# Scaling q and k by the decay factors on GpSimd instead of VectorE, in a fused retention and two-layer feed-forward kernel

## The chip, the cores and the metric

The kernel runs on one core of a Trainium2 chip. A core has five engines with instruction queues of their own: TensorE (PE in the profile; PEld is its weight load), VectorE (DVE), ScalarE (ACT), GpSimd (POOL) and SyncE (SP, which here only issues DMAs). Each engine takes its instructions strictly in the order of its queue, and an instruction that waits for a semaphore holds everything queued behind it. The metric is the device time of one execution in microseconds (us), as the median of several runs.

## The reference

```
scores = q @ k.T / sqrt(64)                    # q, k, v: (4 batches, 8 heads, 576, 64), float32
gamma  = 1 - 2 ** (-5 - arange(8))             # one decay per head
D[i,j] = gamma ** (i - j) if i >= j else 0
x      = ((scores * D) @ v)                    # heads side by side: (2304, 512)
h      = x @ w_in1;  g = where(h > 0, h, exp(min(h, 0)) - 1);  y = g @ w_out1     # 512 -> 2048 -> 512
h      = maximum(y @ w_in2, 0);                out = (h * h) @ w_out2
```

The weights arrive as float64.

## The kernel before, in words

The 2304 tokens are cut into five blocks (512, 512, 256, 512 and 512 tokens), and the blocks into 20 chunks of at most 128 tokens that don't cross a batch: 4, 5, 2, 5 and 4 chunks. The decay gamma^(i-j) is split into a factor for the query and one for the key, so each chunk's q and k (token by 8 heads by 64) are multiplied once by a table `cs` before anything else is done with them: this is `scale_chunk`, L261 to L269, two TENSOR_TENSOR instructions of 128x512 (or 64x512) in place for each chunk. In the kernel before, the 4 chunks of the first block are scaled on GpSimd and the other 16 on VectorE.

A chunk then goes through three pieces (`attn_pieces`). `transposes` turns q and k on TensorE into PSUM (`ps_t`, L293), and ScalarE copies them out (`qT`, `kT`, L298). `scores` multiplies them (`ps_s`, L306), and VectorE applies the causal mask (`P`, L309). `values` adds the state of the earlier chunks (`ps_o`, L321) and the products with v (L325); ScalarE and VectorE split the result into a high and a low part `x` (L159, L160); the state `st` is brought up to date from `ps_u` (L335, L341, L343).

All large products are made of three float32r products of high and low parts (`mm3`, L163 to L165). The first layer is `up` (`h`, then L365 to L370 and the split of `g`) and `down` (`acc`). Its weights are turned from float64 to float32 on the chip (`to_f32`, L204 and L205 on ScalarE, L206 to L211 on VectorE) and split (`w`, L159 and L160). Blocks 0 and 1 share each weight tile as it is made, so that from 14 us to about 90 us of the trace the attention of blocks 0 and 1, the making of the weights and the first products lie side by side. The attention of blocks 2, 3 and 4 is spread between the products of blocks 1 to 3, up to some 410 us. The second layer follows (`A`, `D`, L492; then `m`, L675); no scaling is done in it.

q, k and v of a chunk come in by DMAs from SP's queue (L256) into buffers that two chunks share in turn; a load waits there until the chunk two before is through with its buffer.

The order of each engine's instructions isn't the order of the source: a scheduler sorts them when the kernel is built, by priorities and its own model of when each engine is free. Taking instructions off one engine therefore moves others on all engines.

Of the kernel before, what the change touches and what calls it, by code (L numbers as in the profile page):

```python
# [85 lines left out]
def chunks_of_blocks():  # L86


    out = []
    for t, n in BLOCKS:  # L90
        end, cs = t + n, []
        while t < end:
            b, s = divmod(t, S)
            n = min(P, S - s, end - t)
            cs.append((b, s, n))
            t += n
        out.append(cs)
    return out
# [6 lines left out]
def scale_cols(s):  # L105
    c = C_S + 2 * H * STARTS.index(s)
    return c, c + H
# [19 lines left out]
def tile_kernel(ctx: ExitStack, tc, q, k, v, w_in1, w_out1, w_in2, w_out2, cst, out):  # L127
    nc = tc.nc
# [109 lines left out]
    blocks = chunks_of_blocks()  # L238
# [22 lines left out]
    def scale_chunk(ch):  # L261
        n = ch[2]
        qn, kn, _ = nat[ch]

        eng = nc.gpsimd if ch in blocks[0] else nc.vector
        for t, c in zip((qn, kn), scale_cols(ch[1])):
            eng.tensor_tensor(
                out=t[:n], in0=t[:n], in1=cs[:n, c:c + H].unsqueeze(2).to_broadcast([n, H, D]), op=ALU.mult
            )  # L269

# [450 lines left out]
    def scale_next():  # L721
        if at["scale"] < at["load"]:
            scale_chunk(chunks[at["scale"]][0])
            at["scale"] += 1
# [184 lines left out]
```

## Time and profile before

| | |
|---|---|
| median of 3 runs | 890.87 us (886.36 to 891.96) |
| the profiled execution | 890.54 us, of which the span of the profile is 888.7 us |
| TensorE busy | 857.8 us, 97% of the span |
| VectorE busy | 685.7 us, 77% |
| ScalarE busy | 490.6 us, 55% |
| GpSimd busy | 8.7 us, 1%, 12 instructions |

TensorE is busy nearly all the time, so what counts are the stretches in which it has to wait, or runs at a lower clock. Busy shares are means over stages that differ; the rows below are taken from the stages in which the scaling is done.

### The profile page before, as it was taken

To read this page: it belongs to the slowest core of one execution; us is meant where nothing else is said; L and a number is where in the kernel's file an instruction comes from. 1 tells how busy PE (TensorE), PEld (TensorE's weight loads), DVE (VectorE), ACT (ScalarE), POOL (GpSimd) and SP (SyncE) were. 2 spreads that over 40 slices of the span, in tenths; PEclk is the share of its full clock that TensorE was granted. 3 is DMA by queue.
4 is the path that set the end of the run, shared out by engine and by line. 5 is a ranking of instruction groups with operands and counts; after the bars stand their busy time and mean duration, and the time that the engine had idled before them with its cause. 6 is when DMAs were issued, how large, how long until landed. Compare 5 with 4: busy or idle time off the path is not lost.

```text
span 888.7 us, 14956 instructions
## 1 busy us (share of the span) xinstructions
PE 857.8 (97%) x5630; PEld 771.3 (87%) x5630; DVE 685.7 (77%) x1391; ACT 490.6 (55%) x961; POOL 8.7 (1%) x12
## 2 busy tenths in 40 slices
PE   7898999999998999999999999999999989999998
PEld 5686888888887988888888898999989989999997
DVE  4998888885666868766778867789884769898984
ACT  3674778673464656555767744556553434444441
POOL 3000000000000000000000000000000000000000
PEclk9999899999999999999999999999999999999999
DMA  9944306383529656533462034499998994444330
GB/s 226 276 107 160 96 24 190 119 214 95 142 63 221 163 157 185 187 107 131 142 225 95 25 104 157 154 328 332 348 319 281 401 345 137 160 146 144 120 131 37
DMA packets 157608, 155.33 MB, mean 175 GB/s; under 512 B 62816, under 2 KB 121312, under 8 KB 157536
## 3 DMA queue, kind: packets, MB, share of 16 engines
q1 hardware_dynamic: 150208, 139.69, 51.9%
q10 hardware_dynamic: 7328, 14.68, 4.6%
q8 instruction: 44, 0.72, 0.3%
q14 instruction: 28, 0.23, 0.1%
HBM read 98.77 MB, written 55.57 MB: 174 GB/s over the span
## 4 chain that ended last, share of the span: by engine, by line
PE 73%; DVE 10%; DMA 9%; issue 3%; ACT 2%; SPq 2%; ACTq 0%; DVEq 0%
PE m L675 18%; PE acc L163 7%; PE acc L164 7%; PE acc L165 7%; PE h L163 7%; PE h L164 6%; PE h L165 6%; PE A L492 5%; PE D L492 3%; DMA k<-in_k_dram 2%; DMA f<-w2s 2%; PE ps_o L325 2%; DVE go L519 1%; DMA wo2s<-wo 1%; PE ps_o L321 1%
## 5 line engine op out<-in xcount | busy, mean ns | idle before, releaser
L675 PE MATMUL m<-wo,S 128*128 128x256 f32 x1512 | 183.8, 284 | 3.6 <-ACT S L159 3.6
L675 PEld LDWEIGHTS m<-wo,S 128*128 128x128 f32 x1512 | 183.3, 193 | 4.0 <-ACT S L159 4.0
L159 ACT CAST S<-g 128x512 fp32r<-128x512 f32 (+1 forms) x144 | 75.3, 565 | 94.2 <-DVE g L659 45.6
L163 PE MATMUL h<-x,w 128*128 128x512 f32 (+1 forms) x320 | 120.3, 378 | 3.4 <-DVE t L370 2.4
L165 PE MATMUL h<-x,w 128*128 128x512 f32 (+1 forms) x320 | 118.8, 371 | 0.0
L164 PE MATMUL h<-x,w 128*128 128x512 f32 (+1 forms) x320 | 118.7, 371 | 0.0
L164 PE MATMUL acc<-g,w 128*128 128x512 f32 (+1 forms) x320 | 118.5, 371 | 0.0
L165 PE MATMUL acc<-g,w 128*128 128x512 f32 (+1 forms) x320 | 117.5, 370 | 0.0
L492 PE MATMUL A<-T,pair 128*128 128x384 f32 x576 | 113.4, 336 | 1.5 <-DVE go L519 0.8
L163 PE MATMUL acc<-g,w 128*128 128x512 f32 (+1 forms) x320 | 111.4, 375 | 2.2 <-DVE x L402 1.3
L492 PEld LDWEIGHTS A<-T,pair 128*128 128x128 f32 x576 | 100.5, 188 | 4.0 <-DVE go L519 2.3
L160 DVE TENSOR_TENSOR S<-g,S 128x512 fp32r<-128x512 f32 (+1 forms) x144 | 86.4, 621 | 22.7 <-ACT S L159 20.9
L365 ACT ACTIVATE t<-h 128x512 f32<-128x512 f32 (+1 forms) x80 | 44.3, 554 | 82.5 <-PE h L165 78.9
L369 DVE SCALAR_TENSOR_TENSOR t<-e,t 128x512 f32<-128x512 f32 (+1 forms) x80 | 50.8, 635 | 49.3 <-ACT t L367 49.0
L163 PEld LDWEIGHTS h<-x,w 128*128 128x128 f32 x320 | 60.6, 190 | 15.5 <-DVE t L370 3.4
L159 ACT CAST g<-t 128x512 fp32r<-128x512 f32 (+1 forms) x80 | 46.2, 578 | 47.0 <-DVE t L370 45.2
L163 PEld LDWEIGHTS acc<-g,w 128*128 128x128 f32 x320 | 59.4, 188 | 13.4 <-DVE x L402 1.7
L165 PEld LDWEIGHTS h<-x,w 128*128 128x128 f32 x320 | 60.7, 190 | 10.6 <-DVE w L160 0.2
L164 PEld LDWEIGHTS h<-x,w 128*128 128x128 f32 x320 | 60.7, 190 | 10.2
L164 PEld LDWEIGHTS acc<-g,w 128*128 128x128 f32 x320 | 60.3, 188 | 10.2
L165 PEld LDWEIGHTS acc<-g,w 128*128 128x128 f32 x320 | 60.2, 188 | 10.1
L492 PE MATMUL D<-T,pair 128*128 128x384 f32 x288 | 58.5, 336 | 1.7 <-DVE pair L160 1.1
(88 smaller groups left out, 1279.3 us busy)
## 6 DMA issues: line engine op xcount, KB each, us to landing
g2s<-go SPq DMA_DIRECT2D x48, 384.0 KB, 4.4
g<-g2s SPq DMA_DIRECT2D x36, 512.0 KB, 3.7
raw<-in_moe_w_in_dram SPq DMA_DIRECT2D x32, 512.0 KB, 5.6
raw<-in_moe_w_out_dram SPq DMA_DIRECT2D x32, 512.0 KB, 4.3
wo2s<-wo SPq DMA_DIRECT2D x56, 256.0 KB, 4.2
wo<-wo2s ACTq DMA_DIRECT2D x9, 1536.0 KB, 14.8
w2s<-f SPq DMA_DIRECT2D x32, 256.0 KB, 2.2
f<-w2s SPq DMA_DIRECT2D x32, 256.0 KB, 3.9
```

The costliest lines, as they stand in the source:

```text
L159: nc.scalar.copy(pair_hi, src)
L160: eng.tensor_tensor(out=pair_lo, in0=src, in1=pair_hi.bitcast(F32), op=ALU.subtract)
L163: nc.tensor.matmul(ps, l_hi, r_hi, start=first, stop=False)
L164: nc.tensor.matmul(ps, l_hi, r_lo, start=False, stop=False)
L165: nc.tensor.matmul(ps, l_lo, r_hi, start=False, stop=last)
L321: i = nc.tensor.matmul(ps[:, p, :n], st[:, p, :], qT[:, p, :n], start=p == 0, stop=True, skip_group_check=True)
L325: nc.tensor.matmul(ps[e * D:(e + 1) * D, p, :n], vn[:n, 2 * p + e, :], live[e][:n, p, :n], start=not s, stop=True, skip_group_check=True,)
L365: nc.scalar.activation(t, h, AF.Relu, scale=-1.0)
L369: nc.vector.scalar_tensor_tensor(out=t, in0=e, scalar=1.0, in1=t, op0=ALU.add, op1=ALU.mult)
L492: ins = nc.tensor.matmul(ps, w[:, l, o:o + P], t[:, r, j], start=first and i + j == 0, stop=i + j == 3, skip_group_check=True)
L519: nc.vector.tensor_tensor(out=out, in0=by3(x), in1=by3(y), op=ALU.add)
L675: ins = nc.tensor.matmul(m(u, k), l[:, x], w[:, y], start=first and k in (1, 6, 4, 5), stop=j == HF - 1 and i == 2, skip_group_check=True,)
```

## The change

The choice of an engine goes, and all 20 chunks are scaled on GpSimd:

```diff
-        eng = nc.gpsimd if ch in blocks[0] else nc.vector
         for t, c in zip((qn, kn), scale_cols(ch[1])):
-            eng.tensor_tensor(
+            nc.gpsimd.tensor_tensor(
                 out=t[:n], in0=t[:n], in1=cs[:n, c:c + H].unsqueeze(2).to_broadcast([n, H, D]), op=ALU.mult
             )
```

32 instructions leave VectorE's queue and stand in GpSimd's, behind the 8 that were there, in the order of the chunks. The file is one line shorter from here on, so L293 of the kernel before is L292 of the changed one, and so on.

What follows are pieces of the order of instructions, without times. The first is TensorE's, where the third chunk of block 1 gets its scores (`ps_s`, at 68.45 us of the trace) and its values (`ps_o`, at 70.39 us), among the products of the first layer. Before:

```order
L164 MATMUL acc_732<-g,w_435 128x512
L165 MATMUL acc_732<-g,w_435 128x512
L164 MATMUL acc_733<-g,w_435 128x512
L165 MATMUL acc_733<-g,w_435 128x512
L306 MATMUL ps_s<-qT,kT 128x128 x8
L321 MATMUL ps_o<-qT,st 128x128 x4
```

and after:

```order
L164 MATMUL acc_732<-g,w_435 128x512
L305 MATMUL ps_s<-qT,kT 128x128 x8
L165 MATMUL acc_732<-g,w_435 128x512
L164 MATMUL acc_733<-g,w_435 128x512
L165 MATMUL acc_733<-g,w_435 128x512
L320 MATMUL ps_o<-qT,st 128x128 x4
```

Three products of the first layer now stand between the scores and the values.

The second is TensorE's too, between the values of the fourth chunk of block 1 and the transposes of its fifth (at 86.05 us of the trace). Before:

```order
L335 MATMUL ps_u<-v,k 64x64 x8
L165 MATMUL acc_730<-g,w_706 128x512
L165 MATMUL acc_731<-g,w_706 128x512
L165 MATMUL acc_732<-g,w_706 128x512
L165 MATMUL acc_733<-g,w_706 128x512
L293 MATMUL ps_t<-cs,q 128x64 x4
L293 MATMUL ps_t<-cs,k 128x64 x4
```

and after:

```order
L164 MATMUL acc_733<-g,w_706 128x512
L165 MATMUL acc_730<-g,w_706 128x512
L165 MATMUL acc_731<-g,w_706 128x512
L165 MATMUL acc_732<-g,w_706 128x512
L165 MATMUL acc_733<-g,w_706 128x512
L320 MATMUL ps_o<-qT,st 128x128 x4
L324 MATMUL ps_o<-P_789,v 64x128
```

Four products (L165) that stood between the values with their state (`ps_o`, `ps_u`) and the next transposes now stand ahead of the values, and the transposes follow right behind `ps_u`.

The third is VectorE's, in block 2's products, around 297 to 302 us of the trace; `t` (L369, L370) is the activation of the first layer, `k` a chunk of block 3 that is scaled. Before:

```order
L160 TENSOR_TENSOR x<-ps_o,x 128x4x128
L341 TENSOR_TENSOR st<-ps_u,st 64x4x64 x2
L369 SCALAR_TENSOR_TENSOR t<-e,t 128x256
L267 TENSOR_TENSOR k<-k,cs 64x512
L370 TENSOR_TENSOR t<-h,t 128x256
L206 TENSOR_SCALAR f<-f 128x512
```

and after:

```order
L160 TENSOR_TENSOR x<-ps_o,x 128x4x128
L340 TENSOR_TENSOR st<-ps_u,st 64x4x64 x2
L368 SCALAR_TENSOR_TENSOR t<-e,t 128x256
L369 TENSOR_TENSOR t<-h,t 128x256
L206 TENSOR_SCALAR f<-f 128x512
```

The scaling is gone from between the two steps of the activation; nothing has come in its place.

## Rows read from the trace of the kernel before

**Rows 1.** Busy time by stretches: length, then each engine; PEclk is TensorE's granted clock.

```profile
30.00:70.00 40.00, 38.14 (x276) 31.34 (x276) 38.77 (x74) 24.84 (x46) 0.00 (x0) 0.96 0.64 164
70.00:92.00 22.00, 18.08 (x190) 14.89 (x192) 16.33 (x32) 10.52 (x21) 0.00 (x0) 0.95 0.47 156
92.00:97.00 5.00, 5.00 (x20) 3.91 (x17) 4.83 (x11) 2.96 (x6) 0.00 (x0) 0.54 0.00 0
...
760.00:888.70 128.70, 124.41 (x1037) 124.21 (x1036) 104.40 (x239) 51.90 (x100) 0.00 (x0) 1.00 0.36 119
```

**Rows 2.** TensorE's timeline, 40 to 92 us: start, length, what, [idle before, releaser].

```profile
44.79 0.47 PE L163 MATMUL h<-x,w 128*128 128x512 f32 x1 [0.54 <-DVE t L370]
...
70.39 1.16 PE L321 MATMUL ps_o<-qT,st 128*128 128x128 f32 x8 [0.78 <-DVE P L309]
...
79.93 0.50 PE L163 MATMUL acc<-g,w 128*128 128x512 f32 x1 [0.77 <-ACT w L159]
...
86.05 0.43 PE L293 MATMUL ps_t<-cs,q 64*128 64x64 f32 x4 [0.51 <-DVE x L160]
...
89.12 1.36 PE L321 MATMUL ps_o<-qT,st 128*128 128x64 f32 x8 [1.03 <-DVE P L309]
```

**Rows 3.** TensorE's timeline, 280 to 302 us.

```profile
280.26 0.66 PE L293 MATMUL ps_t<-cs,q 128*128 128x128 f32 x4 [1.33 <-DVE x L160]
...
288.76 0.38 PE L163 MATMUL h<-x,w 128*128 128x256 f32 x1 [0.71 <-DVE t L370]
...
301.94 0.39 PE L163 MATMUL h<-x,w 128*128 128x256 f32 x1 [0.48 <-DVE t L370]
```

**Rows 4.** The scaling's own line: count, duration in ns min/median/max, first and last start.

```profile
L267 DVE TENSOR_TENSOR q<-q,cs x16: 677/684/694, 32.1 to 360.4; 128x512 f32<-128x512 f32 x12, 64x512 f32<-64x512 f32 x4
...
L267 POOL TENSOR_TENSOR spare<-spare,cs x6: 1042/1044/1140, 8.7 to 21.1; 128x512 f32<-128x512 f32 x6
```

**Rows 5.** VectorE's timeline, 16 to 21 us.

```profile
16.47 0.74 DVE L206 TENSOR_SCALAR f<-f 128x512 f32<-128x512 f32 x1
17.13 0.68 DVE L309 TENSOR_TENSOR spare<-ps_s,cs 128x512 f32<-128x512 f32 x1
17.73 0.93 DVE L208 SCALAR_TENSOR_TENSOR f<-raw,f 128x512 int32<-128x512 int32 x1
...
19.80 0.91 DVE L211 CUSTOM_DVE_ANT_0 f<-raw,f 128x1024 uint16<-128x1024 uint16 x1
```

**Rows 6.** GpSimd's timeline in the same stretch.

```profile
15.88 2.22 POOL L267 TENSOR_TENSOR spare<-spare,cs 128x512 f32<-128x512 f32 x2 [4.93 <-DMA spare<-in_q_dram]
19.11 1.04 POOL L267 TENSOR_TENSOR spare<-spare,cs 128x512 f32<-128x512 f32 x1 [1.01 <-DMA spare<-in_q_dram]
```

**Rows 7.** Two lines' durations on VectorE, L206 and L208, as in rows 4.

```profile
L206 DVE TENSOR_SCALAR f<-f x64: 405/419/737, 14.5 to 457.0; 128x512 f32<-128x512 f32 x64
...
L208 DVE SCALAR_TENSOR_TENSOR f<-raw,f x64: 673/685/925, 17.7 to 458.4; 128x512 int32<-128x512 int32 x64
```

**Rows 8.** Waits over the whole span: total us, times, longest.

```profile
DVE k L267 <- DMA k<-in_k_dram: 9.1, 7, 3.5
...
DVE q L267 <- DMA q<-in_q_dram: 7.2, 5, 2.7
```

**Rows 9.** VectorE's timeline, 278 to 302 us.

```profile
278.91 0.69 DVE L267 TENSOR_TENSOR q<-q,cs 128x512 f32<-128x512 f32 x1 [2.65 <-DMA q<-in_q_dram]
...
285.23 0.68 DVE L267 TENSOR_TENSOR q<-q,cs 64x512 f32<-64x512 f32 x1 [1.85 <-DMA q<-in_q_dram]
...
300.75 0.68 DVE L267 TENSOR_TENSOR k<-k,cs 64x512 f32<-64x512 f32 x1 [2.16 <-DMA k<-in_k_dram]
301.46 0.42 DVE L370 TENSOR_TENSOR t<-h,t 128x256 f32<-128x256 f32 x1
```

**Rows 10.** TensorE's timeline, two products in a row.

```profile
66.77 0.39 PE L165 MATMUL acc<-g,w 128*128 128x512 f32 x1
67.00 0.39 PE L164 MATMUL acc<-g,w 128*128 128x512 f32 x1
```

## The prediction

> **What bounds the kernel now.** I read the profile in this order: busy time by stretches, TensorE's timeline for its gaps, the scaling's own line, the waits, and then both sides of the first 25 us, the one place where GpSimd and VectorE work side by side.
>
> TensorE bounds the kernel; VectorE matters only where TensorE waits for it. There are two such places. From 30 to 92 us VectorE is busy 38.8 of 40 us and then 16.3 of 22 us [rows 1], and TensorE's gaps end on it, directly or through a weight that it finishes: 0.54, 0.78, 0.77, 0.51 and 1.03 us [rows 2]; with one more like the 0.77 (0.74 us, at 73.77) and one of 0.46 us (at 87.40), neither shown, that is 4.83 us. Right behind them, from 92 to 97 us, the granted clock is 0.54, so TensorE runs there at its lower level, 1.2 of 2.4 GHz, most of the time: 5 us times 0.46 makes 2.3 us lost [rows 1]. Before it fell, TensorE had stopped three times within 4 us. The second place is block 2's products, where gaps of 1.33, 0.71 and 0.48 us end on VectorE [rows 3], 2.5 us together.
>
> So all that VectorE could give back is 4.83 + 2.3 + 2.5 = 9.6 us, 1.1% of the profiled execution's 890.54 us (its span, 888.7 us, and 1.84 us around it). It lies 0.33 us under the median of the three runs, 890.87 us, so a sum against it needs no correction. The three runs lie 5.6 us apart, and about 1%, 8.9 us, is what a measurement of this kernel can tell from no change.
>
> **Taken off VectorE.** 32 instructions, 16 for q and 16 for k [rows 4]: ten for block 1's five chunks, from 32.1 us on, the others in the products of blocks 1 to 3. One takes 0.68 us, but gives way to the next after 0.60 us, as the one of 0.68 us at 17.13 does to that at 17.73 [rows 5]: 6.0 us in the first place, 13.2 us later.
>
> **Put on GpSimd.** The same work takes 1.04 us there [rows 4]; behind the first block's 8 nothing else stands in that queue, which is idle from then on. Such an instruction can start as soon as its DMA has landed; on VectorE it stood in line. The path from a load to the transposes gets longer by 0.36 us (1.04 less 0.68) where TensorE waits for the load itself, which I see only at 280.26.
>
> **What the two do to each other.** This is the price that decides. Two GpSimd instructions run from 15.88 to 18.10 us and one from 19.11 to 20.15 [rows 6]. Beside them VectorE's L206 takes 0.74 us, L208 0.93 and L211 0.91 [rows 5], where the medians of L206 and L208 are 0.42 and 0.685 [rows 7], and L211 is taken to be as long as L208; both L208 and L211 end 0.56 us after GpSimd's end (18.66, 20.71). So they were held until GpSimd was through, and then ran. L309, which takes one input from PSUM, starts at 17.13 in the middle of the pair and keeps its 0.68 us: it isn't held. In the weights' conversion and the activation most instructions are of the first kind (L206, L207, L208, L211, the splits of `w` and `g`, L369). One GpSimd instruction therefore costs VectorE between 0, where it meets nothing of that kind, and 1.04 us, where it holds VectorE for all its time. The rows' own mean: L206 lost 0.32, L208 0.24 and L211 some 0.22 us, together 0.78 over three GpSimd instructions, 0.26 each. VectorE had free time there; in a full queue I take 0.6, between the mean of the rows and the upper end. Against the 0.60 that the instruction cost VectorE itself this is nothing: ten times (0.60 less 0.6) is 0 us in the first place. The ends are 3.4 us won, at 0.26 each, and 4.4 us lost, at 1.04 each.
>
> The Trainium skill, SBUF — State Buffer, section "SBUF: two separate sides", puts this as an exclusive lock: a VectorE instruction with two SBUF inputs, or in a two-port mode, and a GpSimd instruction exclude each other, and the later one waits for the whole of the other. The rows above agree, L309's too. By it the 0.6 would stand nearer to 1.04, and the first place would lose up to 4.4 us, which is the second rival.
>
> **The waits in VectorE's queue that go.** While VectorE waits for a load of q or k, all its other work stands behind: 9.1 us for k and 7.2 us for q [rows 8]. Three of those show in TensorE's gaps. At 285.23 it had stood 1.85 us for q, and at 300.75 it had stood 2.16 us for k with L370 right behind it, at 301.46 [rows 9], for which TensorE then waited, 0.71 and 0.48 us [rows 3]. In the new order nothing stands between the two steps of the activation; both gaps should go: 1.2 us. The wait at 278.91, 2.65 us [rows 9], holds up the split of `x`, and with it the transposes at 280.26. But these need the same q, which GpSimd has at 278.91 + 1.04 = 279.95 at the earliest, so only some 0.2 of that 1.33 us goes. The other 22 instructions of that stage meet a VectorE with free time and cost nothing that TensorE sees. Gain: 1.2 + 0.2 = 1.4 us.
>
> **What the new order moves.** At 70.39 TensorE waits 0.78 us for the masked scores. Three products now lie between scores and values; in a row they start 0.23 us apart [rows 10], 0.69 us: gain 0.7 us. At 86.05 the opposite: four products (0.9 us) that covered the way from values over `x` to the next transposes now stand ahead of the values. They are done either way, but the way itself lies open: I expect the gap of 0.51 us to grow, and count 0.4 us lost net, since the values' own wait at that place gets shorter. The dip of the clock behind it then stays, 0 us. The other gaps of the first place I leave as they are: the 0.77 comes from weights that were made late, and VectorE gets no faster by the balance above.
>
> The order also changes in the last stage (from 760 us), where nothing is scaled. TensorE's idle time there is 4.3 of 128.7 us [rows 1]; another order can take some of that away or double it, 4 us to either side; I count 0.
>
> **Sum:** 890.54 - 1.4 - 0.7 + 0.4 = 888.8 us. Its own range is 883 to 895: the ends of the first place and of the last stage reach 4 us or so to either side each, and are hardly met together, so some 6 us to either side.
>
> **First rival: VectorE's relief counts.** If GpSimd's instructions meet mostly work that they don't hold, VectorE's queue in the first place is shorter by up to 6 us, the weights come in time, the stops from 70 to 90 us go and with them the fall of the clock: up to 9.6 us, 881 us. For it: the rows' mean of 0.26 us, and a VectorE 97% busy ahead of these gaps. Against it: several of the gaps are not a matter of load but of a chain (scores, mask, values), and most of VectorE's work there is of the kind that is held.
>
> **Second rival, slower: the lock in a full queue.** If nearly every GpSimd instruction holds VectorE to its end, each costs 1.04 instead of 0.60: ten times 0.44, 4.4 us, in the stretch from 30 to 92 us, in which VectorE has 1.2 us to spare in the first 40. TensorE waits for the weights and masks that come later; a further stop or two brings a second fall of the clock like that at 92 us, 2.3 us; and of the 22 later ones half meet a busy activation, 11 times 0.44, 4.8 us. Together 11.5 us, 902 us. It decides from the point at which the mean hold exceeds 0.60 us by more than VectorE's free time, 1.2 us over ten, so from 0.72 us each. For it: L208 and L211 were held to the very end. Against it: the waits for loads leave VectorE's queue, and the later stage has room.
>
> That the change does something else than it says is excluded by the order: all 32 stand on GpSimd.
>
> **How the numbers follow.** The forecast gets 0.66, the first rival 0.15, the second 0.19; each rival may fall some 5 us to either side of its time. Faster by over 1% is under 882.0 us: two thirds of the first rival's share and 0.02 of the forecast's, 0.12. Slower by over 1% is over 899.8 us: three quarters of the second rival's share, 0.14. Within 1%: 0.74. From 881 to 901 us leaves out half of the first rival and a little over half of the second, 0.18, and holds all of the forecast.
>
> **What would show it.** In the profile after: 40 GpSimd instructions of L267, of about 1.05 us each, and a GpSimd busy time near 42 us. VectorE's L206 to L211 with longest times near 1.5 us and a higher mean, most of all between 30 and 80 us; if their means stay, the first rival holds. No wait of VectorE for q or k; no gaps of TensorE at L163 behind L370 in block 2's products. The gap between scores and values of block 1's third chunk under 0.2 us, that before its fifth chunk's transposes longer. A second stretch with a clock near 0.5 would speak for the second rival. The prediction is wrong if GpSimd's instructions themselves wait long for VectorE, so that TensorE waits for transposes, or if the last stage changes by more than 4 us.

## The result, and the profile after

The changed kernel takes 895.61 us (median of 7 runs, 893.31 to 898.71); the kernel before, run on the same chip, takes 889.96 us (7 runs, 886.36 to 892.68). The ratio is 1.007, with a 95% interval from 1.005 to 1.009; a second set of runs gave 1.0053 (1.0035 to 1.0072). It is slower by some 5 us, where 888.8 us, slightly faster, was forecast. The time lies 0.6 us beyond the forecast's own range, 883 to 895, and within the wider one, 881 to 901; the sign is wrong. The profiled execution took 893.66 us, with a span of 891.9 us. It is among the fastest of the seven and 3.1 us above that of the kernel before, so the two profiles side by side show only a part of the loss.

In the changed kernel all line numbers from 265 on are one less, so the scaling is L266 and the activation's two steps are L368 and L369. Busy time by stretches, which answers to [rows 1], with one wider stretch around the fall of the clock:

```profile
30.00:70.00 40.00, 36.45 (x251) 29.92 (x252) 36.52 (x62) 23.86 (x44) 15.18 (x9) 0.92 0.62 161
70.00:92.00 22.00, 18.87 (x179) 14.96 (x177) 17.65 (x30) 10.81 (x20) 1.63 (x2) 0.98 0.47 156
92.00:97.00 5.00, 4.27 (x43) 4.02 (x42) 2.28 (x6) 1.18 (x3) 0.00 (x0) 0.50 0.00 0
...
86.00:110.00 24.00, 21.44 (x153) 17.98 (x152) 17.93 (x35) 15.07 (x29) 0.00 (x0) 0.79 0.18 64
```

The last stretch in the kernel before:

```profile
86.00:110.00 24.00, 22.43 (x133) 18.64 (x134) 19.89 (x38) 17.23 (x33) 0.00 (x0) 0.86 0.26 72
```

From 30 to 70 us TensorE has lost 1.7 us of busy time (36.45 for 38.14), VectorE is less busy, and the clock still falls at 92 us. TensorE's timeline names the gaps, as in [rows 2] and [rows 3]:

```profile
38.48 0.50 PE L164 MATMUL h<-x,w 128*128 128x512 f32 x1 [0.31 <-DVE x L160]
...
45.15 0.66 PE L292 MATMUL ps_t<-cs,q 128*128 128x128 f32 x4
47.15 0.63 PE L292 MATMUL ps_t<-cs,k 128*128 128x128 f32 x4 [1.34 <-ACT qT L297]
48.51 0.50 PE L163 MATMUL h<-x,w 128*128 128x512 f32 x1 [0.73 <-DVE t L369]
...
82.95 0.50 PE L163 MATMUL acc<-g,w 128*128 128x512 f32 x1 [0.52 <-ACT w L159]
...
89.38 0.43 PE L292 MATMUL ps_t<-cs,q 64*128 64x64 f32 x4 [1.04 <-DVE x L160]
90.15 0.43 PE L292 MATMUL ps_t<-cs,k 64*128 64x64 f32 x4 [0.33 <-DVE st L340]
...
92.75 1.97 PE L320 MATMUL ps_o<-qT,st 128*128 128x64 f32 x8 [0.73 <-DVE P L308]
...
284.28 0.66 PE L292 MATMUL ps_t<-cs,q 128*128 128x128 f32 x4 [1.24 <-POOL q L266]
...
286.17 0.66 PE L292 MATMUL ps_t<-cs,k 128*128 128x128 f32 x4 [0.29 <-POOL k L266]
...
292.69 0.39 PE L163 MATMUL h<-x,w 128*128 128x256 f32 x1 [0.64 <-DVE t L369]
```

The place to look at is 47 to 48.5 us. Before, TensorE transposed q there, waited 0.54 us at 44.79 and went on with `h`'s products; k's transposes came 12 products later. TensorE's timeline of the kernel before:

```profile
43.60 0.66 PE L293 MATMUL ps_t<-cs,q 128*128 128x128 f32 x4
...
47.64 0.60 PE L293 MATMUL ps_t<-cs,k 128*128 128x128 f32 x4
```

Now k's four transposes stand right behind q's. They wait 1.34 us until ScalarE has copied qT out, and then `h` waits 0.73 us for the activation: 2.07 us for 0.54. The gap of 0.78 us at 70.39 is gone, as forecast, and so is the one at 301.94.

The scaling's own line now stands on GpSimd (minimum, median, maximum in ns):

```profile
L266 POOL TENSOR_TENSOR q<-q,cs x17: 1037/1109/2616, 4.6 to 364.7; 128x512 f32<-128x512 f32 x13, 64x512 f32<-64x512 f32 x4
L266 POOL TENSOR_TENSOR k<-k,cs x17: 1039/1138/4648, 6.4 to 371.1; 128x512 f32<-128x512 f32 x13, 64x512 f32<-64x512 f32 x4
```

VectorE's timeline, changed kernel. In the first three rows it is held by GpSimd; the other seven are what it does while TensorE stands at 47 us:

```profile
31.39 1.27 DVE L206 TENSOR_SCALAR f<-f 128x512 f32<-128x512 f32 x1
...
34.73 1.52 DVE L160 TENSOR_TENSOR w<-f,w 128x512 fp32r<-128x512 f32 x1
36.17 1.53 DVE L208 SCALAR_TENSOR_TENSOR f<-raw,f 128x512 int32<-128x512 int32 x1
...
44.97 0.41 DVE L206 TENSOR_SCALAR f<-f 128x512 f32<-128x512 f32 x1
45.31 0.67 DVE L211 CUSTOM_DVE_ANT_0 f<-raw,f 128x1024 uint16<-128x1024 uint16 x1
45.91 0.67 DVE L368 SCALAR_TENSOR_TENSOR t<-e,t 128x512 f32<-128x512 f32 x1
46.51 0.41 DVE L207 TENSOR_SCALAR f<-f 128x512 int32<-128x512 int32 x1
46.85 0.67 DVE L160 TENSOR_TENSOR w<-f,w 128x512 fp32r<-128x512 f32 x1
47.45 0.41 DVE L160 TENSOR_TENSOR x<-ps_o,x 128x256 fp32r<-128x256 f32 x1
47.78 0.67 DVE L369 TENSOR_TENSOR t<-h,t 128x512 f32<-128x512 f32 x1
```

The activation's two steps in the kernel before:

```profile
42.14 0.69 DVE L369 SCALAR_TENSOR_TENSOR t<-e,t 128x512 f32<-128x512 f32 x1 [0.55 <-ACT t L367]
...
43.98 0.67 DVE L370 TENSOR_TENSOR t<-h,t 128x512 f32<-128x512 f32 x1
```

GpSimd's timeline, changed kernel, beside VectorE's first three rows:

```profile
29.78 1.04 POOL L266 TENSOR_TENSOR q<-q,cs 64x512 f32<-64x512 f32 x1 [7.34 <-DMA q<-in_q_dram]
31.24 1.14 POOL L266 TENSOR_TENSOR k<-k,cs 64x512 f32<-64x512 f32 x1 [0.42 <-DMA k<-in_k_dram]
34.30 1.40 POOL L266 TENSOR_TENSOR q<-q,cs 128x512 f32<-128x512 f32 x1 [1.93 <-DMA q<-in_q_dram]
35.66 1.49 POOL L266 TENSOR_TENSOR k<-k,cs 128x512 f32<-128x512 f32 x1
```

So there are two suspects. VectorE's first three rows say lock: four GpSimd instructions from 29.8 to 37.2 us stretch three of VectorE's by 0.85, 0.84 and 0.84 us against the medians of [rows 7] and the 0.68 that a split of `w` takes: 2.53 us, 0.63 for each. The other seven say order: none is longer than usual, but in place of four scalings eight more steps of the weights' conversion stand ahead of the activation in VectorE's row. Its first step had started at 42.14 us before, and starts at 45.91 now.

One thing isn't the change's. The profiled run of the kernel before had a granted clock of 0.83 from 30 to 40 us, as two other profiled runs of this study had (e_bare, o_first); all the rest had 0.61 to 0.68:

```profile
30.00:40.00 10.00, 9.07 (x79) 7.72 (x80) 9.85 (x22) 4.08 (x9) 0.00 (x0) 0.83 0.97 251
```

The same stretch of a kernel that still scales block 1 on VectorE (e_late, below):

```profile
30.00:40.00 10.00, 8.79 (x74) 7.70 (x75) 9.24 (x20) 4.23 (x8) 0.00 (x0) 0.67 1.00 243
```

`h` starts at 35.65 us in the first, 36.88 in the second, 36.83 after the change. Of the delays between the two profiles, 1.2 us is this.

### The profile page after: what moved, and what is told of

Same layout as the page of the kernel before. It is cut to its first block, busy times and chain, and to the rows that moved or that the text cites. A ratio compares the mean times of both kernels' runs of the same rounds, so it can differ in the third digit from the quotient of the medians.

```text
span 891.9 us, 15018 instructions
## 1 busy us (share of the span) xinstructions
PE 862.3 (97%) x5630; PEld 775.5 (87%) x5630; DVE 683.7 (77%) x1359; ACT 490.8 (55%) x961; POOL 53.0 (6%) x44
## 4 chain that ended last, share of the span: by engine, by line
PE 85%; DVE 7%; DMA 3%; issue 2%; ACT 1%; SPq 1%; POOL 0%; ACTq 0%; DVEq 0%
PE m L674 18%; PE A L491 11%; PE acc L163 7%; PE acc L164 7%; PE acc L165 7%; PE h L163 7%; PE h L165 7%; PE h L164 7%; PE D L491 5%; PE B L491 3%; PE ps_o L324 2%; PE ps_o L320 1%; PE ps_s L305 1%; DMA g<-g2s 1%; DVE f L208 1%
## 5 line engine op out<-in xcount | busy, mean ns | idle before, releaser
L165 PE MATMUL h<-x,w 128*128 128x512 f32 (+1 forms) x320 | 118.9, 372 | 0.0
L165 PE MATMUL acc<-g,w 128*128 128x512 f32 (+1 forms) x320 | 117.3, 370 | 0.0
L368 DVE SCALAR_TENSOR_TENSOR t<-e,t 128x512 f32<-128x512 f32 (+1 forms) x80 | 54.3, 678 | 63.0 <-ACT t L366 62.6
L165 PEld LDWEIGHTS h<-x,w 128*128 128x128 f32 x320 | 60.7, 190 | 10.7 <-DVE w L160 0.2
L165 PEld LDWEIGHTS acc<-g,w 128*128 128x128 f32 x320 | 60.3, 188 | 10.3
L160 DVE TENSOR_TENSOR g<-t,g 128x512 fp32r<-128x512 f32 (+1 forms) x80 | 53.8, 673 | 11.8 <-ACT g L159 11.6
```

What stands on the lines that cost most here:

```text
L160: eng.tensor_tensor(out=pair_lo, in0=src, in1=pair_hi.bitcast(F32), op=ALU.subtract)
L165: nc.tensor.matmul(ps, l_lo, r_hi, start=False, stop=last)
L368: nc.vector.scalar_tensor_tensor(out=t, in0=e, scalar=1.0, in1=t, op0=ALU.add, op1=ALU.mult)
```

## The experiments

**Lock or order.** The first two kernels part what the change does (where the scaling runs) from what comes with it (the order of the rows). A function at the end of the tracing ties each engine's instructions to the order that the other kernel had; the scaling's engine is set by itself.

```diff
+        eng = nc.gpsimd if ch in blocks[0] or moved[0] else nc.vector
...
+    def follow(tc, traced, order):
+        dep = mybir.DependencyInfo(mybir.DependencyClass.NoSync, mybir.DependencyReason.DATA)
+        for e, l in order.items():
+            l = [i for i in l if str(traced[i].engine) == e]
+            for a, b in zip(l, l[1:]):
+                tc.add_manual_dep(traced[b], traced[a].name, dep, reason="order")
...
+    for moved[0] in (False, True):
```

That is e_lock: the order comes from the first value, the placement from the second. In e_order the last line has `(True, False)`.

> The placement of the change (GpSimd scales every chunk) with the instruction order of the kernel before on TensorE, VectorE, ScalarE and SyncE; only the 32 scalings are missing from VectorE's row. Theory 1 (GpSimd and VectorE hold each other up where VectorE's queue is full, at 30 to 70 us): the loss is all here, ratio to the kernel before 1.005 to 1.008, with h's first product near 48 us late as in the changed kernel. Theory 2 (the new order costs it, VectorE converting more weights ahead of the activation): ratio 0.998 to 1.000, and VectorE's stretched instructions at 31 to 37 us are still there but cost nothing. Theory 3 (the loss is mostly TensorE's clock at 30 to 37 and 90 to 101 us): 1.002 to 1.004, since the clock's falls follow the small gaps that both orders have.

> The placement of the kernel before (VectorE scales blocks 1 to 4) with the instruction order of the changed kernel on TensorE, VectorE, ScalarE and SyncE, the 32 scalings put into VectorE's row where the scheduler finds room. Theory 1 (lock): ratio to the kernel before 1.000 within 0.2%. Theory 2 (order): 1.004 to 1.007, with the gap ahead of h's product at 48 us that the changed kernel has (0.7 us, and h 3 to 4 us later than before). Theory 3 (clock): 1.002 to 1.004.

e_lock: 1.0014 (0.9992 to 1.0036). e_order: 1.0069 (1.0048 to 1.0090). The order carries the loss, with not one more instruction on GpSimd; the lock theory asked for the opposite. TensorE's timeline in e_lock has the gaps of [rows 2], all of them 1.2 to 1.6 us later, which is mostly the clock's 1.2:

```profile
45.97 0.47 PE L163 MATMUL h<-x,w 128*128 128x512 f32 x1 [0.51 <-DVE t L370]
...
71.94 1.16 PE L321 MATMUL ps_o<-qT,st 128*128 128x128 f32 x8 [0.78 <-DVE P L309]
...
87.50 0.43 PE L293 MATMUL ps_t<-cs,q 64*128 64x64 f32 x4 [0.45 <-DVE x L160]
```

TensorE's and VectorE's timelines in e_order:

```profile
47.08 0.66 PE L293 MATMUL ps_t<-cs,k 128*128 128x128 f32 x4 [0.99 <-ACT qT L298]
48.53 0.50 PE L163 MATMUL h<-x,w 128*128 128x512 f32 x1 [0.79 <-DVE t L370]
```

```profile
45.92 0.68 DVE L369 SCALAR_TENSOR_TENSOR t<-e,t 128x512 f32<-128x512 f32 x1
...
47.80 0.67 DVE L370 TENSOR_TENSOR t<-h,t 128x512 f32<-128x512 f32 x1
```

`h` starts at 48.53 us here and at 48.51 in the changed kernel, and the activation's steps agree to 0.02 us, though here VectorE does the scaling and nothing holds it. The order alone makes that place.

**By block.** Here the scheduler chose the order itself.

```diff
-            nc.gpsimd.tensor_tensor(
+        eng = nc.vector if ch in blocks[1] else nc.gpsimd
+            eng.tensor_tensor(
```

> GpSimd scales blocks 0, 2, 3 and 4; VectorE scales block 1 alone, as before. If the loss lies in block 1, where VectorE's queue is full (theories 1 and 2 both), this keeps only what the later blocks regained: 1 to 2 us faster than before, ratio 0.998. If every scaling on GpSimd costs alike (the rival, lock in every place), 22 of the 32 are still moved and two thirds of the loss stays: 1.004 to 1.005.

> GpSimd scales blocks 0 and 1; VectorE scales blocks 2 to 4 as before. If the loss lies in block 1 (theories 1 and 2): the whole loss or more, ratio 1.007 to 1.009, since nothing is regained later. If every scaling costs alike: a third of it, 1.002 to 1.003.

e_late (above): 1.0006 (0.9987 to 1.0025). e_early, with `nc.gpsimd if ch in blocks[0] + blocks[1] else nc.vector`: 1.0043 (1.0027 to 1.0060). Block 1 carries most of it, but e_early lies below the 1.007 expected for that, and the gain of 0.2% that e_late was to keep isn't there. Their rows fit the order theory: in e_late `h` starts at 45.99 us behind a gap of 0.53, the place as it was before; in e_early k's transposes wait 1.02 us at 47.12 and `h` 0.58 at 48.33, as in the changed kernel.

**Which engine's row.** The changed kernel, with one part of the rows put back: TensorE's alone (e_pe), or all but TensorE's (e_rest). Each pair names a kernel and the rows taken from it.

```diff
+    order, steps = {}, [('before', ('PE',)), ('moved', ('DVE', 'Activation', 'SP')), ('moved', ())]
...
+    order, steps = {}, [('moved', ('PE',)), ('before', ('DVE', 'Activation', 'SP')), ('moved', ())]
```

> The changed kernel with TensorE's row alone put back into the order of the kernel before; VectorE, ScalarE and SyncE keep the order of the changed kernel. The order as a whole carries the loss; this asks which engine's row. Theory A (TensorE's row: k's transposes ahead of h's products let ScalarE's copy of qT show): ratio to the kernel before 1.000 to 1.002, h's first product behind the transposes near 46 us. Theory B (VectorE's row: weight conversions ahead of the activation's two operations): h cannot start before the second of them ends at 48.4, whatever TensorE's row is, so one gap of 2 to 3 us ahead of h, and 1.005 to 1.008.

> The other half: the changed kernel with VectorE, ScalarE and SyncE put back into the order of the kernel before, TensorE's row as the changed kernel has it. Theory A (TensorE's row): 1.005 to 1.007, with the wait of 1.0 to 1.3 us for the copy of qT ahead of k's transposes. Theory B (VectorE's row): 1.000 to 1.002; the activation is done by 45.8 us, h starts at about 47.5 behind k's transposes, and what is left of the loss is the copy's wait less the transposes that need not be done later.

e_pe: 1.0139 (1.0113 to 1.0165). e_rest: 1.0093 (1.0063 to 1.0124). Neither theory holds: each mixture is slower than either whole order. In e_pe the one long gap that theory B asked for is there. In e_rest a wait of theory A's size is there, but it ends on the split of `x`, not on the copy of qT, and `h` waits for nothing. TensorE's timeline of e_pe, then of e_rest:

```profile
48.18 0.50 PE L163 MATMUL h<-x,w 128*128 128x512 f32 x1 [2.54 <-DVE t L370]
```

```profile
46.32 0.79 PE L293 MATMUL ps_t<-cs,k 128*128 128x128 f32 x4 [1.19 <-DVE x L160]
```

So both rows bring a wait of their own, TensorE's ahead of k's transposes and VectorE's ahead of `h`, and the rows of one order are fitted to each other: the share of one engine can't be had by taking it out.

**Relief without lock, lock without relief.** All rows in the order of before.

```diff
+        if ch not in blocks[0] and mode[0] == "bare":
+            return
...
+            if ch not in blocks[0] and mode[0] == "both":
+                for h in (0, H // 2):
+                    i = nc.gpsimd.tensor_tensor(
+                        out=spent[:n], in0=t[:n, h:h + H // 2],
+                        in1=cs[:n, c + h:c + h + H // 2].unsqueeze(2).to_broadcast([n, H // 2, D]), op=ALU.mult
+                    )
```

> Left out: the scaling of q and k in blocks 1 to 4 (32 multiplies), by any engine. All four rows in the order of the kernel before. It gives VectorE the whole relief with no GpSimd beside it. If the lock costs time at all, this beats the kernel with the same order and the scalings on GpSimd (1.0014): 0.995 to 0.997. If neither the lock nor the relief reaches TensorE (the order theory, by which only the rows' order counts), 0.998 to 1.002, the same as that one.

> The kernel before in its own order, VectorE scaling as before, and GpSimd multiplies every scaled q and k of blocks 1 to 4 by the factors once more into a scratch tile that nobody reads (64 multiplies of half the width, so the same GpSimd work as the change brings). It is the lock alone, without relief. Lock theory: ten multiplies in the full stretch at 0.64 us each plus some later, 1.004 to 1.008. Order theory: VectorE's instructions are stretched there, but TensorE's starts move by less than 1 us: 1.000 to 1.002.

e_bare: 0.9981 (0.9963 to 1.0000), above the 0.997 that the lock theory allowed. e_both: 1.0072 (1.0043 to 1.0100). So all that VectorE's relief can give in this order is 0.2%, 1.7 us; and GpSimd beside a VectorE that gets no relief does cost time, as the lock theory said. In e_both `h` waits 0.99 us at 47.70 for the activation instead of 0.51 at 45.97. Not all of that need be the lock: GpSimd's second multiply also keeps the buffers of q and k for longer, so that later loads come later. I didn't part the two. TensorE's timeline of e_bare, whose lines are four further on here than in the kernel before:

```profile
45.29 0.47 PE L163 MATMUL h<-x,w 128*128 128x512 f32 x1 [0.52 <-DVE t L374]
...
70.89 1.16 PE L325 MATMUL ps_o<-qT,st 128*128 128x128 f32 x8 [0.78 <-DVE P L313]
...
80.41 0.49 PE L163 MATMUL acc<-g,w 128*128 128x512 f32 x1 [0.77 <-ACT w L159]
...
89.17 1.10 PE L325 MATMUL ps_o<-qT,st 128*128 128x64 f32 x8 [1.07 <-DVE P L313]
```

**Which place, and the order without scaling.** o_first has the new order up to about 70 us and the old one from there; o_later is its complement; both scale on VectorE. o_bare has the new order throughout.

```diff
+        for e, c in (("PE", 340), ("DVE", 100), ("Activation", 70), ("SP", 300)):
+            for n, e in got[e][:c] if rows == "head" else got[e][c:]:
+                order.setdefault(e, []).append(n)
```

> The placement of the kernel before (VectorE scales blocks 1 to 4). Up to about 70 us all four rows are in the order of the changed kernel, from there on in that of the kernel before. If the order's loss arises in the first place (k's transposes and h's products at 47 us), as the starts of TensorE's products say, the ratio is 1.004 to 1.007, like the whole order's 1.0069. If it arises in all places alike: about half, 1.002 to 1.004.

> The complement: VectorE scales; the rows are in the order of the kernel before up to about 70 us, in that of the changed kernel from there on. First place: 0.999 to 1.002. All places alike: 1.002 to 1.004.

> Left out: the scaling of q and k in blocks 1 to 4, by any engine. All four rows in the order of the changed kernel. It is that order with VectorE's relief and without the lock. If the order costs what it does whatever else VectorE has to do: 1.004 to 1.006 (the order's 0.7% less the relief's 0.2%). If the order costs only because the lock or a full VectorE queue makes its waits long: 0.998 to 1.001, and no wait ahead of k's transposes and h's products at 47 us.

> The changed kernel once more, on the chip of the three others. Order and lock together: 1.005 to 1.009.

o_first: 1.0057 (1.0037 to 1.0077). o_later: 1.0025 (1.0012 to 1.0037). o_bare: 1.0011 (0.9992 to 1.0029). after_again: 1.0053. The first 70 us carry the larger part, but the later places more than nothing. `h` starts behind the transposes at 49.46 us in o_first and at 46.08 in o_later, with 0.1 us between them at `h`'s first product (37.04 and 36.96); 0.66 us of the 3.4 are k's transposes, done early, and 2.6 are lost. TensorE's timeline of o_first, then of o_later, then of o_bare (their lines, too, are four further on):

```profile
48.02 0.66 PE L297 MATMUL ps_t<-cs,k 128*128 128x128 f32 x4 [2.33 <-ACT qT L302]
49.46 0.80 PE L163 MATMUL h<-x,w 128*128 128x512 f32 x1 [0.78 <-DVE t L374]
```

```profile
46.08 0.47 PE L163 MATMUL h<-x,w 128*128 128x512 f32 x1 [0.53 <-DVE t L374]
```

```profile
49.66 0.66 PE L297 MATMUL ps_t<-cs,k 128*128 128x128 f32 x4 [0.92 <-ACT qT L302]
```

The wait for the copy is longer in o_first than in the other kernels with this order (1.34 us in the changed kernel, 0.99 in e_order), and o_first pays for it twice: from 49.46 to 52.6 us its granted clock is 0.50, TensorE's lower level, and its products start 0.43 us apart instead of 0.23. The other two profiles show no such fall there.

In o_bare the wait for the copy stays and the one for the activation is gone. Its 1.0011 lies between the two expectations: with a relieved VectorE the new order costs less, about 0.3% against e_bare.

The traces also say how much of the order's loss this place holds. With GpSimd scaling in both, the changed kernel runs behind e_lock by 2.5 us at `h`'s start behind the transposes (48.51 and 45.97; 0.6 of it are k's transposes, done early), by 3.1 us at the 201st product of `h` and `acc` together, behind the dip of the clock (114.44 and 111.31), and by 4.3 us at the first product of `A`; in after_again by 3.0, 3.6 and 4.8. e_lock, then the changed kernel:

```profile
509.53 1.23 PE L492 MATMUL A<-T,pair 128*128 128x384 f32 x6
```

```profile
513.79 1.23 PE L491 MATMUL A<-T,pair 128*128 128x384 f32 x6
```

Each is one execution. So the place at 47 us is the largest single piece, under half of the whole, and 1.1 to 1.2 us arise only behind 110 us, in the products of blocks 1 and 2; what does it there stays open.

The two causes side by side (ratio to the kernel before):

| order of the rows | VectorE scales | GpSimd scales | scaling left out |
|---|---|---|---|
| of the kernel before | 1 | 1.0014 | 0.9981 |
| of the changed kernel | 1.0069 | 1.0070, 1.0053 | 1.0011 |

Along a row, from VectorE to GpSimd, almost nothing happens: +0.1% in the old order, 0 or -0.2% in the new. Down a column the new order costs 0.7%, 0.4 to 0.6% and 0.3%.

## Why the prediction was wrong

- **What bounds the kernel** was right: TensorE, held up by VectorE in the first place. But the 9.6 us that VectorE could give back were far too many: with the scaling taken away altogether, in the old order, it was 1.7 us. Nor is about 1% the least that a measurement of this kernel can tell: the measured 0.7% has an interval of 0.5 to 0.9%. Four of the five gaps in [rows 2] stayed in e_bare, at 0.52, 0.78, 0.77 and 1.07 us; they are chains, not load, as the prediction had held against its first rival, which is out.
- **The price of a GpSimd instruction**, 0.6 us for a VectorE instruction of 0.60 saved, nothing net, was right: 0.63 each in the four from 29.8 to 37.2 us; the six later ones of block 1 cost VectorE 0, 0.25, 0.84, 0.86, 0.65 and 0.84 us, so that the mean of all ten is 0.60. The whole move, with the order held fixed, measured +0.1%. That the mean came out so exactly is luck: 0.6 was a pick between two bounds, and single ones cost either 0.25 us and less or 0.65 and more. The Trainium skill, SBUF — State Buffer, section "SBUF: two separate sides", has the later of the two wait for the whole of the other; the trace agrees (the L208 of 36.17 us ends at 37.70, GpSimd's instruction beside it at 37.15), but e_lock shows that net of the relief little of it reaches the end. Against e_bare, GpSimd's scaling costs 0.33%, 2.9 us, and VectorE's own 0.19%, 1.7 us, each uncertain by about as much as the difference. The second rival is out as well: its 4.4 us in the first place aren't in e_lock's rows.
- **The waits for loads**, 1.4 us forecast: 0.35 came. The gap at 301.94 went (0.48). That at 288.76 only fell from 0.71 to 0.64: an L211 stands between the activation's two steps there, as it did before (at 287.69), and in place of the load VectorE's queue waits 4.82 us for ScalarE's part of a weight (L206 at 289.32). That at 280.26 fell from 1.33 to 1.24 and now ends on GpSimd's q, with 0.29 us more for its k. The gap of 1.27 us at 270.45, which the prediction hadn't named, fell to 0.74 (at 274.69): 0.48 + 0.07 + 0.09 - 0.29 = 0.35 us, and 0.88 with this one. Over all, the changed kernel is 4.6 us behind the kernel before at the 201st product (114.44 and 109.86) and 3.2 behind at the first of `A`, so 1.4 us were won back in between: the forecast's size, but by luck, since the places that it named give a quarter of it.
- **The order: the step that failed.** The prediction took two places from the new order, -0.7 and +0.4. Both came as told: the 0.78 went, and the 0.51 at 86.05 became 1.04 with 0.33 for k behind it. But of the rest it said "The other gaps of the first place I leave as they are". That is the error. The same new order puts k's transposes ahead of 12 products, so that ScalarE's copy of qT is no longer covered, and eight more steps of the weights' conversion ahead of the activation, so that `h` waits for it: 2.07 us of waiting for 0.54, and 2.6 us lost in o_first against o_later. The order term was taken as -0.3 us; it measured 0.69% of 889.6 us, +6.1 us (4.3 to 8.0) with VectorE scaling, and with GpSimd scaling 0.4 to 0.6%, 3.5 to 5 us. Under half of that stands at 47 us, and a part in the products of blocks 1 and 2, for whose order the prediction took only the waits that go. The difference between two orders was read where the old trace had gaps, not where the new one would open some.
- **The dip of the clock** at 92 us stayed, but was not the 0 us that was counted: from 86 to 110 us the granted clock is 0.79 in both profiles of the changed kernel and 0.86 in the kernel before, by the prediction's own way of counting 1.7 us more (24 us times 0.07; an estimate, and an upper one, since TensorE stands still in a part of it). In e_order and e_lock it is 0.86, one execution each, so neither the order nor the placement alone shows it. The last stage, counted at 0, gave 0: from the first product of `A` (510.58 and 513.79 us) to the end of the span it is 378.1 us in both profiles.

What stays open: why the scheduler chose that order. Its planner sees VectorE with room and fills it with weights; that is argued from the rows, not shown. How the order's loss of 0.7% divides between TensorE's row and VectorE's can't be told from mixtures that are slower than both. And no version here beats the kernel before by more than 0.2%: even without any scaling the interval ends at 1.0000.

## What to carry over

Where a scheduler sets the order, moving work to another engine is two changes: the work's place, and a new order for everyone. Hold one fixed and measure the other before arguing about contention; here the contention was plain in the profile and cost almost nothing net, while the order made the loss. In a comparison of two orders, ask of each moved piece what it used to cover: twelve products that stood between two sets of transposes were the cover of a copy.

## Not expected of the hardware

The hold works both ways. GpSimd's multiply, 1.04 us at its shortest, takes 2.62 and then 4.65 us in GpSimd's timeline of the changed kernel:

```profile
45.81 2.62 POOL L266 TENSOR_TENSOR q<-q,cs 128x512 f32<-128x512 f32 x1 [8.66 <-PE ps_t L292]
48.39 4.65 POOL L266 TENSOR_TENSOR k<-k,cs 128x512 f32<-128x512 f32 x1
```

From 45.91 to 52.66 us VectorE runs one instruction behind the other, each at its usual 0.41 or 0.67 us; the next two take 0.93 and 1.53. With both queues full GpSimd got no turn for some 3.6 us (4.65 less 1.04), so the side that is ahead can keep the other out for many instructions, not only for one. When it got its turn fits the rows: 1.04 us before their ends, 48.43 and 53.04, is 47.39 and 52.00, and there VectorE comes to instructions with an input from PSUM (the split of `x` at 47.45 and L369 at 47.78; L369 at 52.06), the kind that the prediction found not to be held. In e_both a pair of half multiplies took 5.57 us in one place. It cost nothing here: TensorE's timeline lists no gap between 48.51 and 77.08 us.
